# One transform as four 64x64 pieces, 33 PSUM copies and 27 transfers moved to other queues, and a new order of the whole program

## The chip, the cores and the metric

The kernel runs on one core of a Trainium2 chip. The core has engines that run side by side, each working through its own list of instructions in order: TensorE (PE, matrix products into PSUM), VectorE (DVE), ScalarE (ACT), GpSimd (POOL) and SyncE (SP). POOL and SP do little here but issue DMA transfers; POOL's go through the software queue q0 and SP's through the hardware queue q1 of the page, and all share 16 DMA engines. Engines wait for one another by semaphores. PSUM, where matmuls leave their results, has 8 banks of 128x512 f32; a bank can be used again when its content has been copied out ("evicted") to SBUF.

The metric is the device time of one execution in microseconds (us), lower is better. The kernel before took 361.94 us (median of three runs: 360.91, 361.94, 363.68).

## The reference

Two independent halves are computed from 2048x1024 bf16 inputs and set side by side in the output. Cut to what matters:

```python
# half A: short convolution, gate, long convolution by FFT of length 4096, gate
for t in range(4):
    k_shift += k_pad[:, t:t+S, :] * shift_k[:, 3 - t]
kv  = k_shift * v
y_f = rfft(kv padded to 2S) * rfft(ssm_k padded to 2S)   # along the sequence, per channel
y   = irfft(y_f)[:S] + kv * ssm_D
a   = q * y
# half B: a diagonal complex state space
Lam_bar = exp(dt * Lam);  Bu = x @ B_bar.T
h[t] = Lam_bar * h[t-1] + Bu[t]                          # 2048 steps, 1024 complex states
b   = 2 * real(h @ C.T) + x * Dskip
```

"The filter" is `ssm_k`, 1024 channels of 2048 taps.

## The kernel before, in words

**Half B** is cut into 16 chunks `i` of 128 time steps. `U(i, jp, jl)` (L422 to L432) is 16 matmuls of 128x128 by 128 columns, 128 such words in all; `ue` (L434) evicts them. On VectorE follow, per chunk, `r1` (a rotation by a table, L447), `r2` (L454), two scans `sc` (L460), `r3` (L447 again) and `r4` (L466). `cy` (L456, ScalarE) copies the carry from the chunk before between `r2` and `sc`. `y(i, dh, part)` (L468 to L479) multiplies the states with C: 4 matmuls of 512 columns and one of 128; 128 words. `ye` (L485) evicts and `yst` (L487, POOL) stores 256 KB. Ahead of it the B matrices are loaded (`bl`), transposed on PE (`bT`, L392) and copied (`bc`, L408).

**Half A** does the FFT as 128 x 32 in two stages. The short convolution on VectorE is `kvm`, `kva`, `kvb`, `kvc` (L511 to L526) for 16 residues `n2`. First stage of the data: `am` (L531), `ae` (L537, eviction), `ast` (L540, store to a DRAM scratch). First stage of the filter: `hl` loads 128 channels, `hT` transposes (L553) eight 128x128 blocks, `hc` (L558) copies them, `hd` (L563) adds `ssm_D` to tap 0, `hm(hf, s, e)` (L565 to L569) multiplies a 128x512 block with two 128x128 matrices `F1t` that hold the transform of the even and of the odd rows, with zeros in the other rows; `he` (L575) evicts, `hst` (L578) stores. There are 32 words `hm`, hence 64 matmuls of 512 columns. Second stage: `lh`, `lk` (L587) load both spectra, `lw` (L582) the coefficients; `sh`, `sk` (L598) are 4 matmuls of 64x64 by 512 columns each, evicted by `she` (L607) and `ske` (L614). `sw` (L618) exchanges even and odd partitions of the filter's spectrum by a DMA from SBUF to SBUF, two per pair `i` of groups, 32 in all, issued by POOL. `pr` (L624, VectorE) multiplies the spectra, `sa` (L636, 8 matmuls of 64x64) transforms back, `sae` (L644) evicts, `vst` (L647) stores. Last stage: when all 16 `vst` have landed, `vl` (L652, SP) loads, `a3` (L664, 2 matmuls) transforms, `a3e` (L671) evicts, `qm` (L673, VectorE) multiplies with q, and `ost` (L674, POOL) stores.

What sets the order is a list of 1486 words written out by hand, `ORDER`. A word names a task, its indices and, behind the colon, the places in SBUF (`a`), the PSUM banks (`p`) and other slots that it takes. The program walks through the list once and appends each task's instructions to the engines' queues; so each engine's own order, and which bank is waited for, are both fixed by the list. All PSUM evictions of the listed kinds are on ScalarE. The functions `swp`, `ysp` and `osp` (the same transfers issued by SP) exist but are not used before.

Of the kernel before, what the change touches and what calls it, by code (L numbers as in the profile page):

```python
# [16 lines left out]
BF16 = mybir.dt.bfloat16  # L17
# [15 lines left out]
def a_constants():  # L33
# [5 lines left out]
    F1 = np.stack([tr * (m % 2 == p)[:, None] for p in range(2)], axis=1)  # L39
    G = np.stack([tr.T * (m % 2 == p)[None, :] * 2 / NFFT for p in range(2)], axis=1)  # L40
# [23 lines left out]
    return f(F1), f(G), f(W)  # L64
# [5 lines left out]
kvm.2:a28 kvm.1:a32 kva.2 kvm.3:a36 par_rest kva.3 kva.1 bl.0.0:a26 kvb.3:a27 bT.0.0:p3 bl.3.1:a40 bc.0.0 bT.3.1:p1 bc.3.1 kvb.1:a52 bT.1.1:p5  # L70
bl.0.1:a41 bT.0.1:p4 bc.0.1 bc.1.1 bl.7.0:a42 bT.7.0:p7 bc.7.0 bl.3.0:a43 bT.3.0:p0 bl.6.1:a44 bT.2.1:p2 bT.6.1:p6 bl.7.1:a45 bc.6.1 bT.7.1:p3
bl.1.0:a46 bT.1.0:p1 sin2 bc.1.0 x.1:a47 x.0:a26 ld_F U.1.0.0:a24p4 U.1.3.0:p5 bl.2.0:a48 kvb.2:a49 kp.-2 bc.2.1 bc.7.1 kvm.0:a8 bc.3.0 bl.5.1:a50
vp.1:a40 eo stt kva.0 bl.4.1:a51 kvc.2 bl.5.0:a42 U.0.0.0:a44p7 U.0.0.1 kvb.0:a43 U.1.0.1 bT.2.0:p6 U.0.3.0:p1 ue.0.0 U.0.3.1 bc.2.0 gz bl.4.0:a46
U.1.3.1 bT.4.1:p2 bT.5.1:p3 bT.5.0:p0 cl.3.0:a48 bT.4.0:p7 U.0.1.0:p6 ue.0.3 bc.4.1 bc.4.0 bc.5.1 U.0.1.1 bc.5.0 U.1.1.0:p1 z1 U.0.2.0:p2 U.0.2.1
# [90 lines left out]
def full_kernel(ctx, tc, A_q, A_k, A_v, A_shift_k, A_ssm_k, A_ssm_D, B_x, B_Lre, B_Lim, B_Bre, B_Bim,  # L165
                B_Cre, B_Cim, B_log_dt, B_Dskip, out):
    nc = tc.nc
# [195 lines left out]
    def wbc():  # L363
        st["wbc"] = sb(4).rearrange("p (j d) -> p j d", j=4)
# [375 lines left out]
```

## Time and profile before

| | |
|---|---|
| three timed runs | 360.91, 361.94, 363.68 us, median 361.94 |
| span of the profiled execution, first to last instruction | 361.0 us; the page gives no other time of its own for this execution |
| PE busy | 336.3 us (93%), 3692 instructions |
| VectorE busy | 315.9 us (88%), 249 |
| ScalarE busy | 282.1 us (78%), 538 |
| POOL busy | 83.1 us (23%), 135 |
| DMA | 100.87 MB, mean 279 GB/s; q1 57.3% and q0 32.0% of the 16 engines' span |

The span leaves out what lies around the first and the last instruction; the median of the runs is 0.9 us above it. "Busy" of an engine is the union of its instructions' durations. PE's matmuls are pipelined, so their durations overlap and a matmul's own duration is longer than the step to the next. Steps are therefore read from starts in the timeline. In the views by stretch, "(x53)" is a number of instructions.

### The profile page before, as it was taken

Reading aid. Unit: us, or ns where it says so; the run is one execution under the profiler, and the core shown is the slowest. Engines: PE = TensorE matmul, PEld = TensorE weight load, DVE = VectorE, ACT = ScalarE, POOL = GpSimd, SP = SyncE. Lnnn points to the kernel's source line nnn. Section 1 sums busy time; section 2 is a strip of 40 time slices with the busy share of each in tenths; the row PEclk is TensorE's granted clock in tenths of the full one; section 3 lists DMA queues with packets and bytes.
Section 4 is the critical chain, followed back from the end, with each engine's and each line's share of the span. In section 5 each row is a group of like instructions: output and inputs, shape, how many; then the busy total and the mean of one; then the engine's idle time right before and its main releaser. Section 6 shows DMA issues by size and latency. Waiting matters only on the chain.

```text
span 361.0 us, 8993 instructions
## 1 busy us (share of the span) xinstructions
PE 336.3 (93%) x3692; PEld 227.0 (63%) x3721; DVE 315.9 (88%) x249; ACT 282.1 (78%) x538; POOL 83.1 (23%) x135
## 2 busy tenths in 40 slices
PE   4398999999999999999999999989999999999992
PEld 1397989654766888476556468455665685664440
DVE  5899799999999999999999977897949868985871
ACT  4799998775657999997767949999999998227561
POOL 6000010040422232363040031231321322100232
PEclk9999999999999999999999999999999999999998
DMA  6999999588499699999879989989998999699974
GB/s 199 295 273 307 276 305 191 89 297 217 154 334 281 255 263 249 272 262 304 305 266 406 272 281 263 321 327 307 314 342 272 294 337 317 243 320 354 349 278 186
DMA packets 61477, 100.87 MB, mean 279 GB/s; under 512 B 29390, under 2 KB 31454, under 8 KB 61436
## 3 DMA queue, kind: packets, MB, share of 16 engines
q1 hardware_dynamic: 49148, 58.21, 57.3%
q0 software_dynamic: 12288, 42.09, 32.0%
q8 instruction: 29, 0.48, 0.6%
q14 instruction: 12, 0.10, 0.1%
HBM read 52.05 MB, written 33.55 MB: 237 GB/s over the span
## 4 chain that ended last, share of the span: by engine, by line
PE 42%; DVE 21%; DMA 12%; issue 10%; ACT 9%; POOL 2%; SPq 2%; POOLq 0%; DVEq 0%; ACTq 0%
PE bank L432 15%; PE bank L476 14%; DVE gslot L460 5%; DVE arena L447 4%; DVE arena L511 4%; DMA arena<-Vs 3%; DMA arena<-arena 3%; ACT arena L607 3%; DMA arena<-in_A_k_dram 3%; PE bank L531 2%; ACT BT L408 2%; PE bank L664 2%; PE bank L569 2%; DVE arena L518 2%; PE bank L598 2%
## 5 line engine op out<-in xcount | busy, mean ns | idle before, releaser
L432 PEld LDWEIGHTS <-BT 128*128 128x128 bf16 x2048 | 117.7, 98 | 13.8 <-issue 5.5
L432 PE MATMUL bank<-arena,BT 128*128 128x128 bf16 x2048 | 124.6, 219 | 1.0 <-ACT BT L408 0.7
L476 PE MATMUL bank<-CT,gslot 128*128 128x512 bf16 x486 | 121.1, 379 | 2.6 <-DVE gslot L466 0.7
L476 PEld LDWEIGHTS <-gslot 128*128 128x128 bf16 x512 | 45.5, 98 | 50.8 <-issue 4.7
L460 DVE TENSOR_TENSOR_SCAN gslot<-rtab,gslot 128x1040 bf16<-128x1040 f32 x32 | 73.0, 2311 | 3.3 <-ACT gslot L456 3.1
L447 DVE TENSOR_TENSOR arena<-arena,Z 128x4096 bf16<-128x4096 bf16 x16 | 36.5, 2284 | 16.2 <-ACT arena L434 16.2
L434 ACT CAST arena<-bank 128x512 bf16<-128x512 f32 x64 | 39.8, 646 | 9.6 <-PE bank L432 6.4
L537 ACT CAST arena<-bank 128x512 bf16<-128x512 f32 x64 | 36.7, 645 | 7.1 <-PE bank L531 6.8
L624 DVE TENSOR_TENSOR arena<-arena 128x4096 bf16<-128x4096 bf16 x16 | 36.3, 2288 | 5.5 <-DMA arena<-arena 2.6
L575 ACT CAST arena<-bank 128x512 bf16<-128x512 f32 x64 | 36.3, 687 | 4.5 <-PE bank L569 2.3
L447 DVE TENSOR_TENSOR arena<-gslot,Z 128x4096 bf16<-128x4096 bf16 x16 | 36.6, 2288 | 1.1 <-DVE gslot L460 0.5
L607 ACT CAST arena<-bank 128x512 bf16<-128x512 f32 x64 | 34.8, 658 | 3.4 <-PE bank L598 3.4
L614 ACT CAST arena<-bank 128x512 bf16<-128x512 f32 x64 | 37.1, 681 | 0.0
L644 ACT CAST arena<-bank 128x512 bf16<-128x512 f32 x64 | 35.2, 674 | 0.9 <-PE bank L636 0.8
L578 POOL DMA_DIRECT2D Ys_h<-arena x32 | 23.0, 725 | 49.5 <-ACT arena L575 45.2
L485 ACT CAST arena<-bank 128x512 bf16<-128x512 f32 x32 | 19.1, 608 | 17.5 <-PE bank L479 17.4
L511 DVE TENSOR_TENSOR arena<-arena 128x4096 bf16<-128x4096 bf16 (+3 forms) x16 | 30.0, 1882 | 1.5 <-DMA arena<-in_A_k_dram 1.5
L671 ACT CAST arena<-bank 128x512 bf16<-128x512 f32 x32 | 17.1, 605 | 17.8 <-remote 9.7
L618 POOL DMA_DIRECT2D arena<-arena x32 | 17.0, 536 | 60.0 <-ACT arena L607 39.6
L479 PE MATMUL bank<-Dd,arena 128*128 128x128 bf16 x128 | 28.0, 219 | 0.0
L598 PE MATMUL bank<-arena,wslot 64*64 64x512 bf16 x256 | 20.7, 386 | 1.5 <-DMA wslot<-a_c_W 1.3
L479 PEld LDWEIGHTS <-arena 128*128 128x128 bf16 x128 | 12.5, 98 | 15.1
(96 smaller groups left out, 378.0 us busy)
## 6 DMA issues: line engine op xcount, KB each, us to landing
Ys_kv<-arena POOLq DMA_DIRECT2D x16, 512.0 KB, 5.4
Ys_h<-arena POOLq DMA_DIRECT2D x32, 256.0 KB, 3.7
arena<-Ys_h SPq DMA_DIRECT2D x16, 512.0 KB, 6.0
arena<-Ys_kv SPq DMA_DIRECT2D x16, 512.0 KB, 5.4
arena<-arena POOLq DMA_DIRECT2D x32, 256.0 KB, 4.4
Vs<-arena POOLq DMA_DIRECT2D x16, 512.0 KB, 5.0
arena<-Vs SPq DMA_DIRECT2D x16, 512.0 KB, 8.7
arena<-in_A_k_dram SPq DMA_DIRECT2D x8, 512.0 KB, 5.7
```

What stands on the lines that cost most here:

```text
L432: nc.tensor.matmul(pu[:, w, jl, :], BT[:, 2 * jp + jl, w, d, :], xT[:, d, :], start=(d == 0), stop=(d == ND - 1))
L434: E["ue"] = lambda i, jp: nc.scalar.copy(st["u", i][:, :, 2 * jp:2 * jp + 2, :], st.pop(("pu", i, jp)))
L447: nc.vector.tensor_mul(m, s_, win(Z))
L460: nc.vector.tensor_tensor_scan(gf, rtab[:].rearrange("p j t -> p (j t)"), gf, 0.0, ALU.mult, ALU.add)
L476: nc.tensor.matmul(py, h[:, w, j, 2:GW], CT[:, j, w, dh * 512:(dh + 1) * 512], start=(j == 0 and w == 0), stop=False)
L479: nc.tensor.matmul(py[:, part * P:(part + 1) * P], st["xT", i][:, d, :], Dd[:, d, :], start=False, stop=(part == 3))
L511: nc.vector.tensor_mul(m[:, 0:h0, :], kring_[:, s0:s0 + h0, :], wbc_[:, 0:h0, :])
L537: nc.scalar.copy(st["ysb", n2][:, p, dh * 512:(dh + 1) * 512], st.pop(("pa", n2, p, dh)))
L575: nc.scalar.copy(st["yh", hf, s][:, p, e, :], st.pop(("pb", hf, s, e, p)))
L607: nc.scalar.copy(st["hab", i][:, 0, a, l, :], st.pop(("ps", "h", g, l)))
L614: nc.scalar.copy(st["x16", i][:, a, l, :], st.pop(("ps", "k", g, l)))
L624: nc.vector.tensor_mul(hab, st.pop(("x16", i)).rearrange("p a l d -> p (a l d)").unsqueeze(1).to_broadcast([P, 2, 2 * D]), hab)
```

## The change

The diff does four things. (1) The filter's first transform, `hm`: instead of two 128x128 matmuls against half-empty matrices, four 64x64 matmuls against one matrix `FQt`, which fill the four quarters of the array: rows 0 to 63 and 64 to 127 of a transposed block now hold the same 64 taps of two different blocks of 128 channels. To feed it, `hT` transposes columns with a step of 32 elements instead of 16, two neighbouring blocks of 128 channels lie in one tile (`hl`), `hd` adds two rows, and `he` writes its 512 columns as four runs of 128. The counts of `hT`, `hc`, `hm`, `he`, `hst` stay 16, 16, 32, 64, 32; PE has 64 instructions more. (2) Evictions named with a `v` run on VectorE: 10 `a3ev`, 8 `saev`, 7 `skev`, 4 `yev`, 2 `shev`, 2 `uev`, which is 33. (3) 14 of the 32 exchanges (`swp`), 8 of 16 `yst` (`ysp`) and 5 of 8 `ost` (`osp`) are issued by SP instead of POOL. (4) The whole list of words has another order, and other places and banks; it has again 1486 words.

```diff
-ld_par ld_G par_T:p0 p32 dd exp1 dve2 dve3 sm_pre tabA1:a0a2a4a6 ld_w:a8 wb.1:p1 wb.0:p2 wbc:a12 wbe.0 wb.4:p3 wbe.4 wbe.1 wb.2:p4 wb.6:p5 wbe.6
-kring:a16 wbe.2 exp2 wb.7:p6 rt wb.5:p7 wbe.5 bl.6.0:a52 tabA2 bl.2.1:a24 bT.6.0:p0 bc.6.0 kp.1 sin0 sin1 bl.1.1:a25 wb.3:p2 wbe.3 kp.0 wbe.7 kp.-1
...
-sae.29.0 sa.28:p7p0 sae.28.0 pr.13 sa.26:p5p4 sa.27:p2p6 y.12.1.2 y.12.0.0:p1 U.15.0.0:a20p7 y.12.0.1 y.12.0.2 y.12.0.3 y.12.1.3 sae.27.0:a46
...
-U.15.1.0:p5 ye.12.1 vl.4:a38 a3.4.1:p1 ue.15.0 a3.4.0:p3 cy.14 a3e.4.1:a14 vl.13:a8 ue.15.2 a3.13.0:p7 U.15.1.1 a3e.13.0:a38 a3.13.1:p1 U.15.3.1
...
-y.14.0.3 a3e.10.0 a3.10.1:p7 vl.1:a26 a3e.10.1 a3.9.0:p6 a3.1.1:p0 a3e.9.0 a3e.4.0 a3.1.0:p7 a3e.1.0:a46 r3.15:a32 a3.5.0:p6 r4.15 y.15.0.0:p3 a3e.5.0
-y.15.1.0:p7 y.15.1.1 a3e.5.1 y.15.1.2 y.15.1.3 qm.5 vl.0:a36 a3.0.0:p6 qm.4 ye.14.1:a52 a3.0.1:p5 ost.1 ost.5 qm.2 a3e.15.0 a3e.1.1 a3e.0.0 qm.7
-a3e.0.1 ost.4 ost.7 y.15.0.1 y.15.0.2 ost.2 ye.15.1:a50 qm.0 ye.14.0 y.15.0.3 ye.15.0 yst.14 ost.0 yst.15
+ld_w:a4 ld_par kring:a16 bl.1.1:a0 wb.4:p2 par_T:p0 wb.6:p3 wb.7:p6 wb.0:p7 bl.6.0:a33 bl.7.0:a28 bl.0.1:a29 kp.1 p32
+exp1 wbe.4:a12 dd bl.2.0:a36 wbe.7 bl.6.1:a32 wb.3:p5 wbe.6 wb.5:p1 bl.0.0:a52 wbe.3 x.1:a30 dve2 kp.0 exp2 bl.1.0:a26
...
+pr.13 sae.24.0 sae.29.1:a6 sae.24.1 sae.28.1 y.12.0.0:p4 sae.29.0 sae.28.0 yst.11 y.12.0.1 U.14.1.0:p2 U.14.1.1
+sa.27:p1p3 sa.26:p5p7 r2.13:h2 vst.12 qp.0:a42 U.14.2.0:p6 sae.27.1:a44 vst.14 U.14.2.1 U.15.0.0:a32p3 qp.6:a5
+sae.26.1 U.15.1.0:p0 cy.13 saev.27.0 saev.26.0 vst.13 U.15.2.0:p5 U.15.3.0:p1 y.12.0.2 U.15.2.1 vl.6:a36 vl.1:a26
+vl.4:a2 vl.5:a20 vl.12:a30 ue.14.1 vl.0:a44 vl.7:a28 vl.13:a48 vl.11:a22 ue.14.2 U.15.0.1 sc.13.0 U.15.1.1 y.12.1.0:p7
+U.15.3.1 a3.6.0:p2 ue.15.3 sc.13.1 r1.14:a12 r2.14:h1 y.12.0.3 r3.13:a16 a3.1.1:p6 vl.15:a0 vl.2:a10 r4.13 cy.14
...
+a3.10.1:p7 y.14.0.3 a3e.10.1 a3.9.1:p3 y.14.1.2 r3.15:a40 a3.9.0:p7 a3e.9.0 yev.14.0:a52 r4.15 y.14.1.3 ysp.12 osp.0
+a3e.9.1 ost.2 qm.6 a3.10.0:p7 a3ev.10.0 qm.5 a3.14.1:p5 a3.14.0:p0 a3e.14.1 osp.6 y.15.1.0:p1 a3.2.0:p4 a3.15.0:p7
+ye.14.1 yst.14 a3.2.1:p3 a3.3.0:p2 qm.4 a3ev.14.0 a3e.2.1:a8 osp.5 osp.4 a3ev.15.0 a3ev.3.0 a3e.2.0 a3.3.1:p5 qm.7
+osp.7 a3ev.3.1 qm.1 ost.1 y.15.1.1 y.15.1.2 y.15.1.3 y.15.0.0:p4 y.15.0.1 yev.15.1:a46 y.15.0.2 y.15.0.3 ye.15.0
+yst.15
...
+    FQ = np.concatenate([tr[::2], tr[::2]], axis=0)
...
+    def either(nm, f):
+        E[nm] = lambda *a: f(nc.scalar.copy, *a)
+        E[nm + "v"] = lambda *a: f(nc.vector.tensor_copy, *a)
...
     def hT(hf, s):
-        pt = bank().bitcast(BF16).rearrange("p (e c t) -> p e c t", e=2, c=4)
+        pt = bank().bitcast(BF16).rearrange("p (n c t) -> p n c t", n=4, c=2)
         st["ph", hf, s] = pt
-        for e in range(2):
-            for c in range(4):
-                hv = st["hk", 4 * hf + c].rearrange("q (m s) -> q s m", s=16)
-                nc.tensor.transpose(pt[:, e, c, :], hv[:, 2 * s + e, :], ident[:])
+        for n in range(4):
+            for c in range(2):
+                hv = st["hk", 2 * hf + c].rearrange("q (m s) -> q s m", s=N2)
+                nc.tensor.transpose(pt[:, n, c, :], hv[:, 16 * (n // 2) + 2 * s + n % 2, :], ident[:])
...
     def hm(hf, s, e):
-        for p in range(2):
-            st["pb", hf, s, e, p] = bank()
-            nc.tensor.matmul(st["pb", hf, s, e, p], F1t[:, p, :], st["hT", hf, s][:, e, :], start=True, stop=True)
+        for r in range(2):
+            st["pb", hf, s, e, r] = bank()
+        for a in range(2):
+            for r in range(2):
+                rows, cols = slice(64 * r, 64 * r + 64), slice(64 * a, 64 * a + 64)
+                nc.tensor.matmul(st["pb", hf, s, e, r][cols, :], FQt[rows, cols],
+                                 st["hT", hf, s][rows, 2 * e:2 * e + 2, :], start=True, stop=True)
```

More of the change, by code (lines that the diff above doesn't have):

```diff
@@ L71 @@
[L71 to L74, printed above, removed]
@@ new lines @@
+r4.11 swp.10.0 sk.20:p4p2 vst.6 sk.21:p7p5 ske.21.0:a20 sae.19.0 ske.20.1 sae.19.1 ske.20.0 sw.11.1 sae.18.1
+y.11.1.0:p1 y.11.1.1 vst.8 pr.11 vst.7 y.11.1.2 sw.10.1 r1.12:a12 ske.21.1 y.11.1.3 lw.15:w2 r2.12:h0 sk.31:p3p7
+lh.14:a34 ye.11.1:a25 ske.31.1:a16 sa.23:p2p4 sk.30:p0p6 vst.9 skev.30.1 sh.31:p5p1 ske.31.0 she.31.0:a0 she.31.1
+cy.12 y.11.0.0:p7 sh.30:p6p5 saev.23.0:a4 she.30.1 sa.22:p2p3 x.13:a24 lk.13:a6 lw.12:w1 sae.22.1 pr.10 sae.22.0
+she.30.0 y.11.0.1 ske.30.0 y.11.0.2 sa.20:p3p1 sae.20.0:a44 saev.23.1 sa.21:p0p5 sw.15.1 sc.12.1 sae.21.0 y.11.0.3
@@ L206, in full_kernel @@
     F1t = const.tile([P, 2, P], BF16, name="F1t")
+    FQt = const.tile([P, P], BF16, name="FQt")
     Gt = const.tile([P, 2, P], BF16, name="Gt")
@@ L384, in wbe @@
     def wbe(b):
+        if "wbc" not in st:
+            st["wbc"] = sb(4).rearrange("p (j d) -> p j d", j=4)
         nc.scalar.copy(st["wbc"][:, :, b * P:(b + 1) * P], st.pop(("wb", b)).rearrange("p (d j) -> p j d", j=4)[:, ::-1, :])
@@ L424, in U @@
         if jl == 0:
-            if jp == 0:
+            if ("u", i) not in st:
                 st["u", i] = sb(2).rearrange("p (w j t) -> p w j t", w=2, j=NJ)
@@ L613, in ske @@
             st["x16", i] = sb(2).rearrange("p (a l d) -> p a l d", a=2, l=2)
-        nc.scalar.copy(st["x16", i][:, a, l, :], st.pop(("ps", "k", g, l)))
-    E["ske"] = ske
+        cp(st["x16", i][:, a, l, :], st.pop(("ps", "k", g, l)))
+    either("ske", ske)
     def swap(dma, i, q):
```

277 lines of the change are left out of this document (152 added, 125 removed).

## The prediction

> **What bounds the kernel now.** I read the busy shares first, then the table by stretches (columns: stretch, its length, busy us and instructions of PE, PEld, DVE, ACT, POOL, then PE's granted clock, DMA share, GB/s). I cut it at two ends of `r4` (L466): chunk 8's, at about 204.5, and the last one's, at 344.77.
>
> ```profile
> span 361.0 us, 8993 instructions
> ...
> 0.00:40.00 40.00, 27.40 (x373) 23.93 (x374) 31.33 (x71) 31.63 (x53) 5.50 (x14) 1.00 1.00 270
> 40.00:204.55 164.55, 162.87 (x1768) 113.95 (x1780) 163.47 (x116) 133.88 (x250) 41.43 (x62) 1.00 0.90 260
> 204.55:344.77 140.22, 136.95 (x1508) 84.92 (x1522) 115.35 (x60) 110.27 (x225) 31.53 (x52) 1.00 0.91 311
> 344.77:361.00 16.23, 9.08 (x47) 4.20 (x46) 5.79 (x5) 6.28 (x13) 4.68 (x7) 0.90 0.58 219
> ```
>
> From 40 to 204.55 PE and VectorE are both full: VectorE is idle for 1.1 us in 164.55. From 204.55 to 344.77 PE is full (idle 3.3) and VectorE has 140.22 - 115.35 = 24.9 us of idle time. ScalarE is loaded unevenly there: from 220 to 300 it is busy for 76.63 of 80 us.
>
> ```profile
> 220.00:300.00 80.00, 77.51 (x982) 49.88 (x985) 65.50 (x33) 76.63 (x157) 21.40 (x36) 1.00 0.94 312
> ```
>
> A full PE also streams. In PE's timeline (start, length, line, count) the starts show the steps:
>
> ```profile
> 60.18 0.59 PE L569 MATMUL bank<-arena,F1t 128*128 128x512 bf16 x2
> 60.61 0.67 PE L553 MATMUL bank<-ident,arena 128*128 128x128 bf16 x8
> 61.12 0.59 PE L569 MATMUL bank<-arena,F1t 128*128 128x512 bf16 x2
> 61.56 1.95 PE L432 MATMUL bank<-arena,BT 128*128 128x128 bf16 x32
> ...
> 183.45 0.22 PE L479 MATMUL bank<-Dd,arena 128*128 128x128 bf16 x1
> 183.60 0.63 PE L598 MATMUL bank<-arena,wslot 64*64 64x512 bf16 x8
> 184.16 1.04 PE L476 MATMUL bank<-CT,gslot 128*128 128x512 bf16 x4
> 185.03 0.22 PE L479 MATMUL bank<-Dd,arena 128*128 128x128 bf16 x1
> 185.09 1.03 PE L476 MATMUL bank<-CT,gslot 128*128 128x512 bf16 x4
> ```
>
> Four matmuls of 512 columns start 0.87 before the next instruction (184.16 to 185.03), so one takes 0.215; one of 128 columns takes 0.06 (185.03 to 185.09).
>
> So two sums are needed, one for each engine that can set the end.
>
> **The filter's transform on PE.** A word `hm` takes 0.43 now (60.18 to 60.61, two matmuls of 0.215); 32 words take 13.8. Four 64x64 pieces on different quarters run at once: L598 above has eight, two groups, in 0.56 to the next start. Of that 0.43 is two groups of 0.215, and together with the 0.09 between 183.45 + 0.06 and 183.60 the remainder is 0.22, lost on going into the small shape and out of it. Thus 32 words stream in 6.9, a saving of 6.9. But each separate run of small pieces pays 0.22. By the two lists, PE has 29 such runs before (`sh`, `sk`, `sa`) and 47 after, 15 of them of `hm`: 18 x 0.22 = 4.0 is given back. Other exits are dearer:
>
> ```profile
> 272.16 0.22 PE L479 MATMUL bank<-Dd,arena 128*128 128x128 bf16 x1
> 272.31 1.15 PE L598 MATMUL bank<-arena,wslot 64*64 64x512 bf16 x16
> 273.54 1.02 PE L476 MATMUL bank<-CT,gslot 128*128 128x512 bf16 x4
> ```
>
> Here 272.31 to 273.54 is 1.23 for four groups of 0.215, and with 0.09 at the entry the run loses 0.46. That is the upper bound, 8.3; an `hm` run has 4 to 12 matmuls and is nearer to the run of 8, so I take 4.0. Net: 2.9 saved on PE. The Trainium skill's "TensorEngine Tiling (Array Packing)", Key Properties, speaks against this part: "Changing tiling mode (not just tile) drains the TensorE". The trace agrees in kind, with the 0.22 us; without a drain the saving would be 6.9, and by the rule it shrinks with every separate run, as counted here.
>
> The 128 transposes stay, with twice the step between elements. Eight of them take 0.51 with the present step (60.61 to 61.12), eight without a step 0.45 (row 55.19 to 55.64 below). A step costs 0.06 per eight; doubling it costs between nothing and, if it doubled the whole step, 16 x 0.51 = 8.2. I take nothing, since the first step already takes every element apart and cost only 0.06.
>
> ```profile
> 55.19 0.61 PE L392 MATMUL bank<-ident,arena 128*128 128x128 bf16 x8
> 55.64 0.68 PE L553 MATMUL bank<-ident,arena 128*128 128x128 bf16 x8
> ```
>
> The evictions `he` and `hc` keep number and size (64 of 0.69, nothing). `hd` becomes four short additions for two, some 0.4 us more on VectorE; the second load of `ssm_D` and that of `FQt` add about 1.1 on POOL, which is 23% busy. I count these as nothing.
>
> **33 evictions on VectorE.** None of this size from PSUM stands in the trace. Nearest are:
>
> ```profile
> L293 DVE SCALAR_TENSOR_TENSOR arena<-arena 128x1024 f32<-128x1024 f32 x1 | 1.2, 1225 | 0.0
> L332 DVE SCALAR_TENSOR_TENSOR Z<-arena,bi 128x128 bf16<-128x128 f32 x8 | 2.7, 340 | 0.0
> L350 DVE COPY rtab<-r 128x1024 f32<-128x1024 f32 x1 | 0.7, 671 | 0.0
> ...
> L614 ACT CAST arena<-bank 128x512 bf16<-128x512 f32 x64 | 37.1, 681 | 0.0
> ```
>
> Between the first two, 512 elements take 340 + 384 x (1225 - 340)/896 = 719 ns, and queued behind another instruction about 70 less (four of 1.22 take 4.66 in the row at 344.68 below): 0.65. A plain copy halves to 0.34 by L350, the low end; 0.72 is the high one. I take 0.65, since the slower rows too read f32 and write 128 partitions, and a PSUM source is no reason to be faster. So 33 cost VectorE 21.5 (11 to 24), 27 of them, 17.6 (9 to 19), ahead of the last `r4`. The Trainium skill's "VectorE: DVE Perf Modes" (the errata section) prices such a copy at 120 + 512 cycles of 0.96 GHz, an estimate of 0.66 us; the sum would be 21.7 in place of 21.5. ScalarE is relieved of 33 x 0.6 = 20, most of it in the stretch where it was full.
>
> **The sum for VectorE.** Counting tasks in both lists, VectorE has the same work ahead of chunk 8's `r4` (the first eviction on VectorE, `saev.7.1`, comes behind it), and the same plus 27 evictions between it and the last `r4`. So, with z for its idle time in the second stretch: 204.5 + 115.4 + 17.6 + z = 337.5 + z. What follows is read from the end of before:
>
> ```profile
> 343.54 1.22 DVE L466 TENSOR_TENSOR gslot<-arena 128x2048 bf16<-128x2048 bf16 x1
> 344.68 4.66 DVE L673 TENSOR_TENSOR arena<-arena 128x2048 bf16<-128x2048 bf16 x4
> ...
> 353.68 0.22 PE L479 MATMUL bank<-Dd,arena 128*128 128x128 bf16 x1
> 353.94 0.59 ACT L485 CAST arena<-bank 128x512 bf16<-128x512 f32 x1 [1.14 <-PE bank L479]
> 354.82 0.58 POOL L487 DMA_DIRECT2D out_dram<-arena  x1 [0.47 <-ACT arena L485]
> ```
>
> From the last `r4` to the end are 16.2 us: PE's last eight `y` words and two `a3`, then eviction, store, landing. In the new list five `a3` lie among those `y`, three more of 0.43: 17.5. VectorE's own rest there (five `qm`, six evictions, 9.9) fits beside. Total 355.0 + z.
>
> **The start** moves by an amount that I only bound. ScalarE and PE waited there for B's loads, since four loads of k went first; chunk 0's rotation waited 2.6 for its last eviction:
>
> ```profile
> 15.31 6.83 PE L392 MATMUL bank<-ident,arena 128*128 128x128 bf16 x80 [5.52 <-DMA arena<-in_B_B_re_dram]
> 16.38 1.94 ACT L408 ACTIVATE BT<-bank 128x1024 bf16<-128x1024 bf16 x2 [2.54 <-PE bank L392]
> 39.74 2.29 DVE L447 TENSOR_TENSOR arena<-arena,Z 128x4096 bf16<-128x4096 bf16 x1 [2.60 <-ACT arena L434]
> ```
>
> The new list loads four B pieces ahead of the first k. At best that saves these 2.5 or so and a little more, 3; at worst the long ScalarE task `eo`, now ahead of most copies of B, costs 2. I take 2 saved. Then VectorE gives 353.0 + z. It was idle for 0.7% in its full stretch and for 18% in the second one. With PE and ScalarE relieved, I take z = 2.5 of 140: 355.5.
>
> **The sum for PE.** 361.0 - 6.9 + 4.0 = 358.1, less 2 at the start. The 3.3 idle us of the second stretch go mostly with ScalarE's load: 2.5 less. One stall comes new: all `vl` wait for the last `vst`.
>
> ```profile
> 302.60 2.01 PE L636 MATMUL bank<-arena,wslot 64*64 64x512 bf16 x32
> 307.66 0.72 POOL L647 DMA_DIRECT2D Vs<-arena  x1 [0.76 <-ACT arena L644]
> 314.73 19.91 SPq L652 DMA_DIRECT2D arena<-Vs  x16
> 321.86 1.46 PE L664 MATMUL bank<-arena,Gt 128*128 128x512 bf16 x5
> ```
>
> From the end of the last `sa` (304.77 by its starts) to the first `a3` are 17.1 us, which PE filled with 19 words of `U` and `y`. The new list has 12 words there, 10.8 us. The round trip needs about 3 for eviction and issue, 5.0 for the store and at least 5 for the load (landing medians 5.0 and 8.7 with a queue of 16), so 13: I charge 2, at most 6. PE: 358.1 - 2 - 2.5 + 2 = 355.6. Both sums meet, which also means that neither engine can hide the other's stalls.
>
> **Exchanges and stores on SP** I count as nothing: transfers and bytes are the same.
>
> ```profile
> POOL arena L618 <- ACT arena L607: 39.6, 9, 16.4
> SPq L582 <- PE bank L636: 62.3, 12, 9.9
> DVE arena L447 <- ACT arena L434: 16.2, 6, 4.8
> ```
>
> POOL, which has nothing behind it but stores, waited 39.6 for the evictions ahead of exchanges. On SP, behind a waiting `swp` stand the loads `lh`, `lk`, `lw`, `x`, which PE needs. SP already waits 62.3 for a free coefficient slot, so its loads are ahead of their use by several us; that is the cover.
>
> **The rivals.** (a) *Slower: VectorE is the wall.* Its queue is in order. An eviction at its head waits for a matmul group, and the next scan and rotation wait behind it, and with them `y`, the next carry and the banks. Place: between chunk 8 and the last `r4`. Its 24.9 idle us of before were waits such as the 16.2 for `ue`; if half stay, z = 12.4 and the time is 353.0 + 12.4 = 365.4. From z = 8 on nothing is won, from z = 12 it is slower by over 1%; all of them kept give 378. Against it: VectorE and PE were full together for 164 us before, in an order of the same kind. (b) *SP's queue.* If each of 14 `swp` holds the loads behind it 0.5 us past their use: 355.5 + 7 = 362.5. (c) *Everything at its low end*: evictions of 0.34 and a start 3 us earlier, VectorE at 355.0 - 3 - 27 x 0.31 + 1 = 344.6, so PE sets it, 358.1 - 3 - 3.3 - 1 = 351 or a little below. (d) *The pieces don't run at once*: 32 x 4 x 0.215 = 27.6 against 6.9 streamed, 376. L598 speaks against it, with the same shape and the same alternation of rows. The dear transposes would give 363.7.
>
> **How the numbers follow.** The profiled span is 0.9 below the median of the runs; I add that: 355.5 + 0.9 = 356.4. Chances: the forecast (353 to 361) 0.50, (c) 0.17, (a) 0.20, (b) 0.10, (d) and the transposes 0.03. The range reaches to (c)'s 351 less 1.5 and into (a), to 367.5. A difference under 1% (358.3 to 365.6) is about what a measurement of this kernel can't tell from no change. Faster by over 1%: (c) and three quarters of the forecast, 0.55. Same: the rest of it, (b) and a part of (a), 0.25. Slower 0.20.
>
> **What would show it.** PE's L569-line: four 64x64 in 0.215, 0.22 lost per run. VectorE's busy time near 338, copies of 0.65 to 0.72. Its idle time between chunk 8's `r4` and the last: under 5 if I am right, over 8 by (a). The first `U` before 20 us. PE's wait for the first `a3`, about 2. ScalarE below 270. SP's waits ahead of `swp`, and PE waiting for loads at L598, tell (b). I am wrong most easily in z, which I chose, and in the start.

## The result, and the profile after

The changed kernel takes 358.59 us (median of 20 runs, 355.66 to 361.57) against 362.47 us for the kernel before on the same chips (20 runs, 360.48 to 367.42): ratio 0.9875, 95% interval 0.9848 to 0.9902. The ratios here are taken without the slowest executions, those over 1.5% above a kernel's fastest, so this one is not quite the quotient of the two medians. The kernel is faster by a little over 1%; 356.4 was forecast. The profiled execution has a span of 355.4 us. It lies at the fast end: its own device time is 357.16 us, 1.8 us more than its span, and other executions of the same kernel had spans from 353.9 to 359.8. So the spans of two single traces of one kernel can differ by several us, and a stretch, too, is told from another only beyond 2 to 3 us; the ratios below are what decides.

The head of its page:

```profile
span 355.4 us, 9118 instructions
...
PE 332.3 (93%) x3754; PEld 223.0 (63%) x3785; DVE 333.8 (94%) x284; ACT 267.2 (75%) x505; POOL 69.7 (20%) x110
```

VectorE went from 315.9 to 333.8 us busy, ScalarE from 282.1 to 267.2. The table by stretches, cut at the same two ends of `r4` (now L499): chunk 8's, at 205.33, and the last one's, at 338.93 (columns as in the prediction):

```profile
0.00:40.00 40.00, 30.33 (x409) 26.79 (x410) 33.49 (x73) 34.89 (x57) 6.48 (x16) 0.91 0.97 280
40.00:205.33 165.33, 159.65 (x1836) 110.05 (x1849) 160.85 (x117) 133.47 (x250) 37.25 (x54) 1.00 0.84 251
205.33:338.93 133.60, 131.38 (x1463) 81.11 (x1475) 130.01 (x88) 95.79 (x195) 24.09 (x38) 1.00 0.97 333
338.93:355.40 16.47, 10.89 (x57) 5.05 (x56) 9.45 (x11) 3.07 (x6) 1.85 (x3) 0.91 0.60 228
20.00:30.00 10.00, 9.13 (x130) 9.13 (x131) 10.00 (x15) 8.48 (x10) 0.00 (x0) 0.75 1.05 356
```

Up to chunk 8's `r4` nothing was won (205.33 against 204.55). Between the two `r4` 6.6 us were: 133.60 for 140.22. VectorE is busy there for 130.01 where it was 115.35, and its idle time fell from 24.9 to 133.60 - 130.01 = 3.6. PE has 45 instructions fewer in that stretch and is busy for 131.38, though the last `hm` runs at 153 us: 39 matmuls of `U` now lie ahead of it, which at 0.056 each is 2.2 us, and 8 of `a3` behind it. ScalarE, at 110.27 before, is down to 95.79. And the column that the prediction did not use, the DMA share, rose from 0.91 to 0.97, with 333 GB/s for 311.

PE's timeline (start, length, line, count, and the idle time before it in brackets), `U` being L462, `hm` L610, `hT` L588:

```profile
13.13 0.61 PE L462 MATMUL bank<-arena,BT 128*128 128x128 bf16 x8 [0.27 <-ACT arena L415]
...
20.87 3.60 PE L462 MATMUL bank<-arena,BT 128*128 128x128 bf16 x32 [4.85 <-ACT BT L438]
24.26 1.83 PE L422 MATMUL bank<-ident,arena 128*128 128x128 bf16 x24
...
118.40 0.63 PE L610 MATMUL bank<-arena,FQt 64*64 64x512 bf16 x8
118.96 1.07 PE L462 MATMUL bank<-arena,BT 128*128 128x128 bf16 x16
119.86 0.68 PE L588 MATMUL bank<-ident,arena 128*128 128x128 bf16 x8
120.38 0.83 PE L462 MATMUL bank<-arena,BT 128*128 128x128 bf16 x12
```

Two words `hm` take 0.56 to the next start (118.40 to 118.96), 0.43 of it streaming and 0.13 on the way out. Eight transposes with the doubled step take 0.52, where the single step took 0.51. VectorE's new evictions, by groups (count, busy us and mean ns) and then one of them in its timeline:

```profile
L714 DVE CAST arena<-bank 128x512 bf16<-128x512 f32 x10 | 6.6, 683 | 0.0
L687 DVE CAST arena<-bank 128x512 bf16<-128x512 f32 x8 | 5.4, 687 | 0.1
```

```profile
210.92 0.68 DVE L687 CAST arena<-bank 128x512 bf16<-128x512 f32 x1
211.52 2.31 DVE L493 TENSOR_TENSOR_SCAN gslot<-rtab,gslot 128x1040 bf16<-128x1040 f32 x1
```

One lasts 0.685, and the next instruction starts 0.60 after its start.

### The profile page after: what moved, and what is told of

Same layout as the page of the kernel before. It is cut to its first block, busy times and chain, and to the rows that moved or that the text cites. A ratio compares the mean times of both kernels' runs of the same rounds, so it can differ in the third digit from the quotient of the medians.

```text
span 355.4 us, 9118 instructions
## 1 busy us (share of the span) xinstructions
PE 332.3 (93%) x3754; PEld 223.0 (63%) x3785; DVE 333.8 (94%) x284; ACT 267.2 (75%) x505; POOL 69.7 (20%) x110
## 3 DMA queue, kind: packets, MB, share of 16 engines
q0 software_dynamic: 9872, 33.74, 26.3%
## 4 chain that ended last, share of the span: by engine, by line
PE 39%; DVE 11%; DMA 9%; issue 5%; ACT 3%; SPq 0%; POOL 0%; POOLq 0%; DVEq 0%
PE bank L509 14%; PE bank L462 13%; DMA wslot<-a_c_W 5%; PE bank L679 4%; DVE gslot L493 4%; PE bank L641 4%; DVE arena L480 4%; DMA arena<-Ys_kv 2%; DMA arena<-in_A_q_dram 2%; ACT arena L593 1%; PE bank L610 1%; PE bank L564 1%; PE bank L512 1%; ACT arena L657 1%; DVE gslot L499 1%
## 5 line engine op out<-in xcount | busy, mean ns | idle before, releaser
L462 PE MATMUL bank<-arena,BT 128*128 128x128 bf16 x2048 | 126.6, 221 | 5.5 <-ACT BT L438 5.2
L462 PEld LDWEIGHTS <-BT 128*128 128x128 bf16 x2048 | 118.3, 99 | 19.2 <-issue 9.1
L509 PEld LDWEIGHTS <-gslot 128*128 128x128 bf16 x512 | 44.7, 98 | 53.2 <-issue 9.4
L467 ACT CAST arena<-bank 128x512 bf16<-128x512 f32 x62 | 37.7, 635 | 13.7 <-PE bank L462 13.6
L618 ACT CAST arena<-bank 128x512 bf16<-128x512 f32 x64 | 34.7, 616 | 10.6 <-issue 4.7
L570 ACT CAST arena<-bank 128x512 bf16<-128x512 f32 x64 | 35.1, 627 | 6.9 <-PE bank L564 6.9
L650 ACT CAST arena<-bank 128x512 bf16<-128x512 f32 x62 | 34.6, 618 | 4.3 <-PE bank L641 4.1
L657 ACT CAST arena<-bank 128x512 bf16<-128x512 f32 x57 | 33.2, 632 | 4.9 <-PE bank L641 4.9
L687 ACT CAST arena<-bank 128x512 bf16<-128x512 f32 x56 | 31.6, 634 | 3.4 <-PE bank L679 2.3
L518 ACT CAST arena<-bank 128x512 bf16<-128x512 f32 x28 | 17.2, 614 | 17.4 <-PE bank L512 13.8
L573 POOL DMA_DIRECT2D Ys_kv<-arena x16 | 11.1, 701 | 72.8 <-ACT arena L570 68.3
L714 ACT CAST arena<-bank 128x512 bf16<-128x512 f32 x22 | 12.2, 595 | 16.5 <-PE bank L707 16.5
L641 PE MATMUL bank<-arena,wslot 64*64 64x512 bf16 x256 | 20.4, 386 | 2.1 <-DMA wslot<-a_c_W 1.1
```

Of the source, the lines that this page charges most:

```text
L462: nc.tensor.matmul(pu[:, w, jl, :], BT[:, 2 * jp + jl, w, d, :], xT[:, d, :], start=(d == 0), stop=(d == ND - 1))
L467: either("ue", lambda cp, i, jp: cp(st["u", i][:, :, 2 * jp:2 * jp + 2, :], st.pop(("pu", i, jp))))
L509: nc.tensor.matmul(py, h[:, w, j, 2:GW], CT[:, j, w, dh * 512:(dh + 1) * 512], start=(j == 0 and w == 0), stop=False)
L570: cp(st["ysb", n2][:, p, dh * 512:(dh + 1) * 512], st.pop(("pa", n2, p, dh)))
L618: cp(o, st.pop(("pb", hf, s, e, r)).rearrange("p (n c t) -> p n c t", n=2, c=2))
L641: nc.tensor.matmul(st["ps", nm, g, l][64 * dh:64 * dh + 64, :], st["w", i][rows, a * WC:a * WC + 64], st[nm, i][rows, a, dh * 512:(dh + 1) ...
```

## The experiments

Line numbers differ a little from kernel to kernel. The starts of three `r4`, read from VectorE's timelines, show where each run gains or loses:

| kernel | chunk 8 | chunk 12 | chunk 15 | ratio to before, 95% |
|---|---|---|---|---|
| before | 203.31 | 287.46 | 343.54 | 1 |
| changed | 204.11 | 284.35 | 337.71 | 0.9875 (0.9848 to 0.9902) |
| changed, `hm` in full size | 205.79 | 288.32 | 342.51 | 1.0008 (0.9981 to 1.0035) |
| changed, all evictions on ScalarE | 204.65 | 289.51 | 345.66 | 1.0136 (1.0085 to 1.0186) |
| changed, exchanges and stores on POOL | 207.56 | 300.03 | 353.19 | 1.0306 (1.0262 to 1.0350) |
| old order, evictions on VectorE | 202.03 | 313.97 | 379.74 | 1.1056 (1.1001 to 1.1110) |
| old order, `hm` in pieces | 201.84 | 285.80 | 340.83 | 0.9973 (0.9949 to 0.9998) |

**Which part carries the gain.** First the new order with one part undone at a time.

The transform again as two 128x128 matmuls per word, on the new layout, against a matrix filled up with zeros:

```diff
-                nc.tensor.matmul(st["pb", hf, s, e, r][cols, :], FQt[rows, cols],
-                                 st["hT", hf, s][rows, 2 * e:2 * e + 2, :], start=True, stop=True)
+            nc.tensor.matmul(st["pb", hf, s, e, r], FQt[:, r * P:(r + 1) * P],
+                             st["hT", hf, s][:, 2 * e:2 * e + 2, :], start=True, stop=True)
```

> The new order with the filter's transform as two full-size 128x128 matmuls per word again (the other half of the matrix holds zeros; the result is the same). My theory: the 64 matmuls take 6.9 us more of PE, 4.0 come back from 15 fewer shape changes, net +2.9 on PE; this part of the program (40 to 205 us) is held by VectorE, so the time rises by 0 to 3 us: ratio to the kernel before 0.988 to 0.996. Rival: the cheaper transform is where the gain comes from; then the whole of it is lost and the ratio is 1.000 or more.

Measured: 362.77 us, ratio 1.0008. The whole gain is gone, a span 4.8 us longer (360.2), and my theory with it. PE is busy for 336.3 us where the changed kernel has 332.3. All of PE's additional work lies before 160 us, in a stretch where VectorE is full too. By its steps that work is 3.6 us (6.9, less 15 runs at 0.22), and the loss is 4.8, or 2.9 to 6.8 by the ends of the two intervals.

How the loss comes about is not settled. In this trace 1.7 us of it show at chunk 8's `r4`, 4.0 at chunk 12's and 4.8 at the last. But in the changed kernel and six further runs below, which all do the same work up to there, chunk 8's `r4` starts anywhere from 202.39 to 205.18. And in the 136.72 us between the two `r4` both engines have the work of the changed kernel and are idle for longer (VectorE 6.4 for 3.6, PE 4.6 for 2.2; PE waits 2.7 for coefficient loads where it waited 1.1). That PE had a lead which is used up first, so that the loss surfaces later, is a reading that no run here shows; the run with `eo` moved, below, speaks against it.

All 33 evictions on ScalarE (each `...v` in the list renamed, so `nc.vector.tensor_copy` becomes `nc.scalar.copy`):

> The new order with all 33 evictions back on ScalarE. My theory: the relief of ScalarE in the second half of the program is what shortened it; VectorE has 27 x 0.60 = 16 us less there, but PE waits for banks again, and the gain of 5.6 us is lost to about nothing: ratio 0.995 to 1.010. Rival: VectorE is the wall, and without the evictions the new order is as fast or faster: ratio 0.988 or below.

Measured: 367.33 us, ratio 1.0136; the direction was foreseen, the size was more than foreseen. The stretch between the two `r4`, and what VectorE waited for in it (total, times, longest):

```profile
205.87:346.88 141.01, 133.89 (x1459) 81.14 (x1471) 114.67 (x61) 107.39 (x219) 24.03 (x38) 1.00 0.93 317
```

```profile
DVE arena L653 <- DMA arena<-arena: 8.4, 4, 3.7
DVE arena L702 <- ACT arena L700: 6.1, 3, 3.5
DVE arena L466 <- ACT arena L453: 4.6, 2, 4.2
```

VectorE's work is back at 114.67 and its idle time at 26.3, spent waiting for ScalarE's copies and for exchanges that follow them. The stretch is again as long as before (141.01 against 140.22). So the 14.7 us that VectorE took over were idle time before, as the prediction held.

The 14 exchanges and 13 stores back on POOL:

```diff
-... ske.8.1 swp.4.1 lk.9:a44 ...
+... ske.8.1 sw.4.1 lk.9:a44 ...
```

(and so for all 14 `swp`; each of the 8 `ysp` becomes `yst`, each of the 5 `osp` becomes `ost`, at the same places of the list).

> The new order with the 14 exchanges and 13 stores that SP issues given back to POOL. My theory: queue of issue costs nothing either way, ratio 0.984 to 0.992, as with the change whole. Rival b of the prediction: SP's waits hold loads back, so without them it is faster by some us, ratio below 0.980. The opposite rival: POOL's in-order waits delay the exchanges, ratio above 0.995.

Measured: 374.35 us, ratio 1.0306. My theory fell: of the three parts this one costs most to undo. VectorE's wait for exchanges from 204 to 350 us, and POOL's timeline ahead of the longest of them (L647 is an exchange, L653 is `pr`):

```profile
DVE arena L653 <- DMA arena<-arena: 8.2, 3, 7.1
```

```profile
268.56 0.52 POOL L647 DMA_DIRECT2D arena<-arena  x1 [4.89 <-DVE arena L466]
272.80 0.54 POOL L647 DMA_DIRECT2D arena<-arena  x1 [3.72 <-ACT arena L636]
...
274.08 0.54 POOL L647 DMA_DIRECT2D arena<-arena  x1
```

By the list the three are `sw.11.0`, `sw.10.0` and `sw.11.1`. The first two, which the changed kernel gives to SP, wait for VectorE and for an eviction; the third stands behind them in POOL's one queue. `pr.11`, which needs it, starts 5.9 us after that issue, at 279.93, having waited 7.1, with everything on VectorE behind it. In the changed kernel `pr.11` waits 0.5, and not for an exchange.

These waits are 8.2 of the 12.0 us by which the stretch between the two `r4` is longer (145.63 for 133.60). The granted clock there is 0.96; the rest of the 12.0, and the 3.5 lost ahead of chunk 8's `r4`, were not traced to a cause.

**The parts alone, in the old order.** The same 33 evictions on VectorE, nothing else changed:

> The kernel before, in its own order, with the same 33 evictions on VectorE and nothing else changed. My theory: the move needs an order made for it; VectorE has 25 us of idle time in the second half to take 20 us, but it takes them at places where it delays scans: ratio 0.995 to 1.010. Rival: the move alone gives the gain, ratio 0.985 to 0.990.

Measured: 400.37 us, ratio 1.1056, a loss of 38 us where a few were expected. The stretch from chunk 8's `r4`, then VectorE's and PE's timelines in one place of it (L620 evicts what L611 computes; L479 is `r4`, L637 is `pr`, L649 is `sa`, which needs it):

```profile
203.00:375.00 172.00, 141.11 (x1488) 84.88 (x1502) 127.39 (x85) 97.39 (x195) 29.52 (x49) 0.92 0.73 248
```

```profile
266.65 0.69 DVE L620 CAST arena<-bank 128x512 bf16<-128x512 f32 x1 [6.39 <-PE bank L611]
267.26 0.68 DVE L627 CAST arena<-bank 128x512 bf16<-128x512 f32 x1
267.85 4.53 DVE L473 TENSOR_TENSOR_SCAN gslot<-rtab,gslot 128x1040 bf16<-128x1040 f32 x2
272.42 2.29 DVE L460 TENSOR_TENSOR arena<-gslot,Z 128x4096 bf16<-128x4096 bf16 x1
274.74 1.23 DVE L479 TENSOR_TENSOR gslot<-arena 128x2048 bf16<-128x2048 bf16 x1
275.88 2.29 DVE L637 TENSOR_TENSOR arena<-arena 128x4096 bf16<-128x4096 bf16 x1
```

```profile
265.92 1.43 PE L611 MATMUL bank<-arena,wslot 64*64 64x512 bf16 x12
...
278.22 1.92 PE L649 MATMUL bank<-arena,wslot 64*64 64x512 bf16 x16 [7.75 <-DVE arena L637]
```

An eviction at the head of VectorE's queue waits 6.39 us for a group that PE reaches only at 265.92. Two scans, a rotation, `r4` and `pr` stand behind it; PE comes to `sa` and waits 7.75 us for that `pr`. Both engines lose in turn: 44.6 us of idle time on VectorE and 30.9 on PE in 172 us. The whole stretch is like this: 42 of VectorE's 44.6 us stand ahead of evictions, and PE's waits for `pr` come to 20.5 in seven. It is the mechanism of rival (a), complete, at a price far above the one worked out there. A part of the price is PE's speed: the granted clock is 0.92 in this stretch and 0.57 from 274 to 282, around the wait shown. By the row above that is at most 0.08 x 172 = 14 us, an estimate.

The pieces alone, on the old layout:

```diff
-            nc.tensor.matmul(st["pb", hf, s, e, p], F1t[:, p, :], st["hT", hf, s][:, e, :], start=True, stop=True)
+                nc.tensor.matmul(st["pb", hf, s, e, r][cols, :], F1t[rows, r, cols],
+                                 st["hT", hf, s][rows, e, :], start=True, stop=True)
```

> The kernel before, in its old order, with each filter word `hm` as four 64x64 pieces at once on the old layout (each output sums over half of the rows only, so half of that sum is left out; evictions, stores and order as before). By the prediction's PE sum: 32 x 0.215 = 6.9 us saved, 15 separate runs of pieces at 0.22 give 3.3 back, so PE gets 3.6 us of lead by 165 us. Theory (a lead of PE is carried along and is worth its size where PE sets the end, as 4.8 us were lost with the full-size transform in the new order): 2 to 4.8 us, ratio 0.986 to 0.995. Rival (VectorE holds the first 200 us and the order was fitted to the old lengths): 0.997 to 1.005.

Measured: 361.17 us, ratio 0.9973, 0.1 to 1.8 us won. That lies in the rival's range, and the interval just reaches my theory's upper end, 0.995. The trace says why my theory's number was too high: I had taken the 15 separate runs of the new list. PE's group of these pieces, and one of them in its timeline:

```profile
L572 PE MATMUL bank<-arena,F1t 64*64 64x512 bf16 x128 | 12.3, 397 | 0.0
```

```profile
103.57 0.41 PE L572 MATMUL bank<-arena,F1t 64*64 64x512 bf16 x4
103.91 1.04 PE L476 MATMUL bank<-CT,gslot 128*128 128x512 bf16 x4
```

In the old order 24 words stand singly and only four pairs side by side, so there are 28 runs. A single word takes 0.34 (103.57 to 103.91), and with the 0.09 on the way in that is 0.43, what the full-size word took. 28 x 0.22 = 6.2 of the 6.9 us are given back, and 0.7 remain. The new order has 15 runs (4 of one word, 5 of two, 6 of three), so 3.6 remain. The Trainium skill's "TensorEngine Tiling (Array Packing)", Key Properties, has the rule behind it, that a change of tiling mode drains TensorE, without a price; here it decides whether the pieces are worth anything.

**What bounds the kernel now.** The prediction's two sums met at 355.5. I tested that with work left out behind chunk 8: on VectorE (`pr` on half of its columns, 13 times), on PE (one of four C matmuls of `y`), and both.

```diff
-        nc.vector.tensor_mul(hab, st.pop(("x16", i)) ... , hab)
+        n = 2 * D if i in (0, 1, 3) else D
+        nc.vector.tensor_mul(hab[:, :, 0:n], st.pop(("x16", i)) ... , hab[:, :, 0:n])
```

```diff
-            for w in range(2):
+            for w in range(1 if i >= 9 and j % 2 else 2):
```

> The changed kernel with VectorE's spectrum product `pr` on half of its columns for 13 of its 16 pairs (half of these products is left out, the rest of the work is the same): about 13 x 1.1 = 14 us less on VectorE, all of it in the stretch ahead of the last r4, nothing less on any other engine. Theory (both sums meet there, PE has 2.2 us of idle time in that stretch): it gains no more than that, 1 to 3.5 us, ratio to the kernel before 0.978 to 0.986. Rival (VectorE alone is the wall): 8 us or more, ratio below 0.967. Rival (PE alone is the wall): no gain at all, 0.986 to 0.990.

> The changed kernel with one of the four C matmuls of each part of `y` left out in chunks 9 to 15 (a quarter of that sum is left out): 56 x 0.215 = 12 us less on PE, behind chunk 8's r4. Theory (both sums meet; VectorE has 3.6 us of idle time in that stretch): the last r4 comes 1 to 3.5 us earlier and the tail is shorter by 1.7 us (8 matmuls of chunk 15), ratio to the kernel before 0.974 to 0.984. Rival (PE alone is the wall): 8 us or more, ratio below 0.967. Rival (VectorE alone): the tail only, 0.982 to 0.988.

> Both at once: half of 13 spectrum products and a quarter of the C sums of chunks 9 to 15 left out, 14 us less on VectorE and 12 us less on PE. Theory (two engines with equal sums, so that only both together move the end): 9 to 13 us beyond the changed kernel, ratio to the kernel before 0.952 to 0.963, clearly more than the sum of the two alone. Rival (one engine is the wall): within 2 us of the better of the two alone.

Measured: 0.9891 (0.9847 to 0.9936) with less on VectorE, 0.9824 (0.9771 to 0.9878) with less on PE, 0.9791 (0.9748 to 0.9835) with less on both. Less on VectorE alone gains nothing, and less on PE alone too little for its interval to leave that of the changed kernel. So neither engine by itself is the wall, as the theory said. But both together win 3 us beyond the changed kernel (0.0084 x 362.5) where it asked for 9 to 13, and so it falls. The 3 us are 1.2 beyond PE's run alone, as the rival with one engine as the wall had it, but the two single runs speak against either engine as that wall: something else stands at the same height. The changed kernel's own chain of waits has, among its longest pieces behind chunk 8, three transfers (start, length, what):

```profile
254.22 6.15 DMA wslot<-a_c_W
...
284.14 4.49 DMA wslot<-a_c_W
...
323.08 5.64 DMA arena<-in_A_q_dram
```

And two candidates showed in the waits of the run with less on both, from 205 to 339 us (L641 is `sh` and `sk`, L625 the load `lw` of a coefficient slot):

```profile
PE bank L641 <- DMA wslot<-a_c_W: 4.6, 4, 1.5
```

```profile
SPq L625 <- PE bank L680: 21.5, 8, 7.1
```

Either the three slots, reloaded only after their last use, hold it, or the transfers themselves do, or the written order holds the engines apart. Two more runs on top of that one, a fourth slot and fewer bytes:

```diff
-    F1t = const.tile([P, 2, P], BF16, name="F1t")
-    FQt = const.tile([P, P], BF16, name="FQt")
+    F1t = wx[:, 0:256].rearrange("p (a k) -> p a k", a=2)
+    FQt = wx[:, 256:384]
...
-    wslots = [... for s in range(NWS)]
+    wslots = [... for s in range(NWS)] + [wx]
```

> The run with half of 13 spectrum products and a quarter of the C sums of chunks 9 to 15 left out (26 us of work gone, only 1 us won over VectorE's alone or PE's alone), now with four coefficient slots in place of three: the loads `lw` take them in turn, the fourth lies where the transforms' tables and the index table were. Theory A (the loop of a slot holds the stretch: the last `sa` of a pair frees it, the next `lw` takes 4 to 5 us to land, then `sh`; SP waited 21.5 + 8.3 us for that, PE 4.6): 4 to 10 us below the run with three slots, ratio to the kernel before 0.950 to 0.968. Theory B (the transfers hold it, the DMA share is 0.97): as with three slots, 0.974 to 0.983. Theory C (neither; the written order itself holds the engines apart): also 0.974 to 0.983.

```diff
-        spd(st[nm, i], Ys.rearrange("(g r) d -> r g d", r=P)[:, 2 * i:2 * i + 2, :])
+        n = D if i < 4 else HD
+        spd(st[nm, i][:, :, 0:n], Ys.rearrange("(g r) d -> r g d", r=P)[:, 2 * i:2 * i + 2, 0:n])
...
-    E["vst"] = lambda i: gpd(Vw[:, 2 * i:2 * i + 2, :], st.pop(("vsb", i)))
+    E["vst"] = lambda i: gpd(Vw[:, 2 * i:2 * i + 2, 0:HD], st.pop(("vsb", i))[:, :, 0:HD])
...
-        spd(st["vv", n2], Vr[n2])
+        spd(st["vv", n2][:, :, 0:HD], Vr[n2][:, :, 0:HD])
```

> The same less work on VectorE and PE, with three slots, and fewer bytes: `lh` and `lk` of pairs 4 to 15, all `vst` and all `vl` move only half of their columns (left out: half of the inputs of the second transform there and half of the middle result), about 9 of the 44.7 MB between chunk 8's r4 and the last. Theory B (the transfers hold the stretch): 5 us or more below the run with the full bytes, ratio to the kernel before 0.950 to 0.967, the DMA share falls below 0.85. Theory A (the loop of a coefficient slot): at most 2 us, by loads that land sooner, 0.971 to 0.981. Theory C (the order): no change, 0.975 to 0.983.

Measured: 0.9734 (0.9697 to 0.9770) with four slots and 0.9690 (0.9645 to 0.9735) with fewer bytes. The stretch between the two `r4`, one row from each run's table: less on both engines, then with four slots, then with fewer bytes.

```profile
205.10:337.44 132.34, 124.54 (x1429) 77.75 (x1441) 116.80 (x86) 97.12 (x198) 24.11 (x38) 1.00 0.97 335
```

```profile
202.61:333.20 130.59, 124.98 (x1431) 78.11 (x1443) 116.66 (x86) 97.28 (x199) 24.04 (x38) 1.00 0.99 342
```

```profile
202.39:331.04 128.65, 124.76 (x1430) 78.36 (x1441) 117.09 (x87) 97.03 (x198) 24.02 (x38) 1.00 0.75 241
```

With 13.2 us of VectorE's busy time and 6.8 of PE's gone, the stretch is 1.3 us shorter than the changed kernel's 133.60, and the transfers are as full as there. Fewer bytes take another 3.7, and the ratio's interval no longer touches that of the run with all bytes. Waits for transfers went with them, from 205 to 339 us: PE's for coefficients fell from 4.6 to 0.4, VectorE's for exchanges from 4.0 to none, while SP waited for a free slot as long as before:

```profile
PE bank L642 <- DMA wslot<-a_c_W: 0.4, 1, 0.4
```

```profile
SPq L625 <- PE bank L681: 21.2, 7, 7.4
```

Four slots alone take 1.8, to a DMA share of 0.99, and there the intervals overlap. So once both engines have less to do, late transfers are shown to be a third limit; for the slots it is likely and not settled. The changed kernel itself was not run with fewer bytes alone: that the transfers hold it too, as a third wall of about the same height, is argued from its DMA share of 0.97. Neither result fell into the range that either single cause was given, and with less of everything PE is still idle for 3.9 us and VectorE for 11.6, for which no one cause stands; the order remains a candidate, and that stays open.

The fourth slot in the whole changed kernel:

> The changed kernel, whole, with the fourth coefficient slot. Theory A: PE's 2.1 us of waiting for `lw` at L641 goes; VectorE has 3.6 us of idle time in that stretch, so 0 to 2.5 us less than the changed kernel, ratio to the kernel before 0.980 to 0.988. Theories B and C: as the changed kernel, 0.985 to 0.990.

Measured: 359.54 us, 0.9910 (0.9873 to 0.9947): nothing won that can be told. So the slots by themselves do not hold the whole kernel.

**The start.** The long ScalarE task `eo`, behind which PE waited 4.85 us, moved back behind the next four copies of B (`bc`; the expectation says five), and `stt`, which needs it, put behind it:

```diff
-tabA2 sin2 eo bT.0.0:p6 U.1.3.0:a28p7 bc.0.0 ... bl.4.1:a5 bc.1.1
+tabA2 sin2 bT.0.0:p6 U.1.3.0:a28p7 bc.0.0 ... bl.4.1:a5 bc.1.1 eo
```

> The new order with one long ScalarE task of the start, `eo`, moved five copies of B back (and `stt`, which needs it, behind it). In the changed kernel PE waits 4.85 us at 16 to 20.9 for such a copy behind `eo`. Theory (what PE saves early is carried along as a lead, as the full-size transform suggested): PE's wait shrinks by 3 to 4.8, the last r4 comes 1 to 4 us earlier, ratio to the kernel before 0.977 to 0.985. Rival (VectorE alone sets the pace from 40 to 205, so PE's early stall costs nothing): ratio 0.985 to 0.990 as with the changed kernel. Rival of loss: VectorE waits for `stt` in its place and chunk 0 starts later: ratio above 0.990.

Measured: 357.39 us, 0.9862 (0.9834 to 0.9891), not to be told from the changed kernel; the rival held. PE's waits of the first 40 us, and the stretch between the two `r4`:

```profile
PE bank L408 <- ACT BT L424: 3.3, 1, 3.3
```

```profile
202.61:338.49 135.88, 131.59 (x1466) 81.02 (x1478) 130.24 (x87) 95.99 (x195) 24.04 (x38) 1.00 0.96 326
```

The 4.85 us became 3.3 at a later place, chunk 8's `r4` came 1.5 us earlier, and the last one 0.8 us later than in the changed kernel; both differences are within what traces of the same work show. With the same work behind chunk 8, the stretch there is 135.88 long for 133.60.

## Why the prediction was right, and where it was not

The sign, the size and the place were right: the gain comes between chunk 8's and the last `r4`, where VectorE's idle time was filled. The forecast span of 355.5 against 355.4 measured is closer than the working deserves, since its terms missed both ways: 205.3 + 115.3 + 14.7 + 3.6 + 16.5 was measured for 202.5 + 115.4 + 17.6 + 2.5 + 17.5. The step from span to runs was mis-sized: I added 0.9, a run takes 1.8 more than its span, and the profiled execution is 1.4 faster than the median. These make the 2.2 us between 356.4 and 358.59.

**The pieces.** Four in 0.215 and 0.22 lost per run were both right, and so was the count of 15 runs. What was off is their worth: "Net: 2.9 saved on PE" is low. In the new order they are worth 4.8 (full-size run) and in the old one about 1; the steps of 15 runs give 3.6. By the prediction's two sums, which meet, undoing them should cost about 3, which the measurement (2.9 to 6.8) just allows. What fell is the expectation for that run, that VectorE holds this part of the program. By what path PE's time counts where VectorE is full stays open.

**The transposes** cost nothing more, as taken: 0.52 against 0.51.

**The evictions.** Taken at 0.65, the step is 0.60 behind a long instruction (0.685 long); VectorE's busy time in the stretch grew by 14.7 where 17.6 were reckoned; 27 steps of 0.60 would be 16.2, and the other 1.5 are not accounted for. Its whole busy time is 333.8 for "near 338". "A PSUM source is no reason to be faster" was right for the length and left the overlap out. The Trainium skill's "VectorE: DVE Perf Modes", errata section, was closer to the length with its 0.66 than to the step.

**The idle time z**, 3.6 for 2.5, within what the forecast allowed. It was chosen and not derived, and the run with `eo` moved, with the same work in the stretch, has 135.88 - 130.24 = 5.6: that it came out so close is partly luck. The wait of rival (a) did not come, but the old order with these evictions shows that it is real: what kept it away is the new order, not the nature of the work. Its price there was 38 us over the kernel before, where the bound of 378 was 16 over.

**The start**, 2 saved, was the wrong step. Chunk 8's `r4` ends 0.8 later in this trace; the seven traces with this start and the same work up to there have it begin at 203.9 in the mean, the three with the old order at 203.31, 202.03 and 201.84. `U` did start early, at 13.13, but PE then waited behind `eo`, which I had seen and put only at the worst end; and with that wait moved, nothing was won either. The first 40 us gave 2.2 us of VectorE's idle time (8.7 to 6.5), and from 40 to 205 it was idle for 4.5 where it had been for 1.1. Its waits up to there:

```profile
DVE arena L480 <- ACT arena L467: 1.8, 1, 1.8
DVE gslot L493 <- ACT gslot L489: 1.4, 1, 1.4
DVE arena L667 <- DMA arena<-arena: 1.1, 1, 1.1
DVE arena L601 <- ACT arena L593: 0.9, 1, 0.9
```

The first falls at 37.75; the other three make 3.4 of the 4.5 us, and what the start gave went into them. Why each of them arose I did not try.

**The round trip through `Vs`**, charged at 2, cost nothing:

```profile
298.03 1.06 PE L679 MATMUL bank<-arena,wslot 64*64 64x512 bf16 x16
...
309.85 0.60 PE L707 MATMUL bank<-arena,Gt 128*128 128x512 bf16 x2
310.29 1.03 PE L509 MATMUL bank<-CT,gslot 128*128 128x512 bf16 x4
```

The first `a3` (L707) starts 10.9 us after the last `sa` (L679) has ended at 299, behind filling work and without a wait.

**SP's queue.** "Nothing" was right for what the move costs. PE's wait for coefficient loads in the stretch:

```profile
PE bank L641 <- DMA wslot<-a_c_W: 1.1, 2, 0.9
```

So rival (b) did not occur. As the move's worth it was wrong. In the new order it is worth 4.3% of the time, since POOL's queue would hold the exchanges.

**Two sums that meet** was right as a size and incomplete as the bound. The row in the prediction already showed the DMA share at 0.91 and 311 GB/s; a stretch 5% shorter with the same bytes had to bring it near 0.96. The transfers should have been the third sum.

## What to carry to other kernels

Where every engine's queue is in order, as here, moving work to an idle engine may pay only together with an order made for it: the same 33 copies cost 38 us in the old list, and putting them back on ScalarE in the new one costs 9.5. Reckon the DMA engines as one of the engines that can set the end, with their own sum by stretch. And before cutting a matmul into small pieces, count the separate runs that they will form: here one piece-group alone gained nothing, two or three side by side did.

## What the hardware showed that I had not expected

After its idle time of 4.85 us PE ran slowly: the 32 matmuls at 20.87 took 24.26 - 20.87 = 3.39, or 0.106 each, where 16 take 0.90, or 0.056 each, at 118.96; the granted clock from 20 to 30 is 0.75. The Trainium skill's "TensorE: Matmul & The Clock Gate", Part 1, says that an idle window of about 3.4 us halves the clock, with 106.7 and 55.6 ns for a matmul of 128 columns; the trace agrees in the two durations. Not every such wait brings the slow clock, though: the kernel before was granted 1.00 over its first 40 us, with 5.52 us of waiting ahead of 15.31. What the slow matmuls cost is not known, since the run with `eo` moved still has them: 24 at 25.44 take 2.38, or 0.099 each.

Over the stretch behind chunk 8 the transfers reached a share of 0.99 at 342 GB/s in the run with four slots, and no run went beyond that. That is no ceiling: from 20 to 30 us of the changed kernel the same columns read 1.05 and 356.

Undoing any one of the three parts in the new order loses at least about as much as the whole change wins over the old one: 4.8, 9.5 and 15.6 us (differences of the ratios times 362.5) against 4.5. The parts do not add, so none has a worth of its own that could be summed.
